# An H3 layer with a gated product, forward and backward: a third weight slab at the start, transposes at fixed places, and a convolution that runs on into the down product

## The chip, the cores and the metric

The kernel runs on one core of a Trainium2 chip. The metric is device time in microseconds (us) of one execution, the median of several. The engines have the profile's names: PE (TensorE, matmuls and transposes), PEld (its weight loads), DVE (VectorE), ACT (ScalarE), POOL (GpSimd) and SP (SyncE, which issues DMAs only). An engine works through its own list of instructions in order; a DMA is issued by an instruction on the list of SP, ACT or POOL.

## The reference

One layer and all its gradients, with 2048 rows, 1024 features (D) and 3584 hidden features (F), in bfloat16:

```python
xn = _layernorm(q)
# A: convolution over the rows
k_shift = sum_t k_pad[:, t:t+S] * shift_k[:, ks-1-t]      # ks = 4
kv = k_shift * v
y = irfft(rfft(kv, 2S) * rfft(ssm_k, 2S))[:, :S] + kv * ssm_D
s = xn * y
# B: gated product
h = (xn @ w_gate) * (xn @ w_up)
g = silu(h @ w_down)
out = q + s * g
```

The outputs are `out` and its gradients for q, k, v, shift_k, ssm_k, ssm_D, w_gate, w_up and w_down, given grad_out.

## The kernel before

Everything is one program whose order is written out by hand. **Stages**, by the trace: 0 to 62 us the layer norm of q and the first units of the gate/up product; to about 512 us the rest of that product with the forward convolution woven into it; to about 700 us the down product with the gates; then the backward products to the end at 1916 us. Only the first three are touched.

**Layer norm and turning.** q comes in chunks of rows, in blocks of 128: (0,1), (1,1), (2,2), (4,4), (8,4), (12,4) as first block and number (L889). `layer_norm` (L565) makes a chunk's statistics on DVE, a square root on ACT (`half_r`, L580), the normalized rows on DVE (L591), and stores them to XNd from POOL's queue. Each block is then turned, by transposes on PE (L597, L608, and L617 in `turn_late`) and a copy on ACT, into XNT, the stationary side of the product. Blocks of chunks 8-11 and 12-15 wait in a list `turn_rows`, which `turn_late` empties after the first block of the next unit (L660).

**Gate/up product.** The weights come in 14 slabs of 256 columns of w_up beside 256 of w_gate (`load_slab`, L547, two DMAs of 512 KB on SP's queue). `gu_unit(sl, b0, n)` (L640) multiplies n row blocks by slab sl: per block 8 matmuls of 512 columns (L656) into one of two PSUM banks of `ps_gu`, a copy on ACT (gut, L658), and a store of gut to GUd from ACT's queue (L72). Later h = up times gate on DVE (hN, L667), its store, its transposes on PE (L689), and a copy on ACT with a store of h transposed. Slabs 0 and 1 are loaded at the start, between the first chunks of rows; the first units alternate between them, as chunks become ready (L927). From slab 2 on, units of four blocks run over all 16.

**Forward convolution.** It is a generator, `conv_forward` (L706), over eight slices (ds) of 128 features. Per slice: transforms of kv (kind 0) and of ssm_k (kind 1), their product, an inverse transform, and a tail of inverse row matmuls (psY, L446) with copies to yf. A transform is matmuls on PE into banks of `ps_cv` (psF), a copy on ACT into SP (L296), and sums on DVE. `fwd4_half` (L249) takes 16 matmuls of 256 columns; `fwd8_half` (L288) 8, with more sums on DVE (`fwd8`, L298). EIGHT (L698) lists the slices and kinds split by eight. `make_pump` (L473) advances the generator: each piece yields a cost, and after every row block `tick` (L944) pumps until the cost done reaches a share of F_TOTAL, set by `cnt` and NT (L942). Within it the order of DVE's instructions is pinned.

**Down product.** `bm_first` (L998) begins the first two row blocks, two matmuls of 512 columns (L994) per 128 hidden features (fc); `late_mm(n)` (L1327) goes on with one such step per n. Accumulators (psbm) lie in `ps_bm` (two) and `ps_bx` (one). `ps_cv` is released ahead of `bm_first`, so all of the convolution's forward transforms must be issued by then. The tail's last four pieces are placed behind steps n = 52, 55, 58 and 61 (L1337). `gate` (L1255) then combines g, y and grad_out on DVE.

Of the kernel before, what the change touches and what calls it, by code (L numbers as in the profile page):

```python
# [19 lines left out]
def build_kernel(  # L20
# [266 lines left out]

    def fwd8_half(x, i, SP, psp, first=None, held=False):  # L288

        pe_us[0] += 0.87  # L290
        for j in range(2):
# [4 lines left out]
            nc.scalar.copy(out=SP[:, :, j], in_=ps[:].rearrange("p s k x -> p s (k x)"))  # L296

    def fwd8(SPs, X, W, C, ahead, late=False):  # L298
# [225 lines left out]
    ps_tr = pool("ps_tr", 1, space=PSUM)  # L524
    ps_gu = pool("ps_gu", 2, space=PSUM)
    ps_st = pool("ps_st", 4, space=PSUM)
# [19 lines left out]

    def load_slab(sl, eng):  # L547
        w = fw.tile([P, DC, 2, SLW], BF16, name="wslab")
        fs = slice(sl * SLW, (sl + 1) * SLW)
        for a, wsrc in ((0, B_w_up), (1, B_w_gate)):  # L550
            last = eng.dma_start(out=w[:, :, a, :], in_=wsrc[:, fs].rearrange("(dc p) f -> p dc f", p=P))
# [11 lines left out]
    turn_rows = []  # L563

    def layer_norm(b0, n, x4):  # L565
# [22 lines left out]
        for i in range(n):  # L588
            b = b0 + i
            q, qi = divmod(b, 4)  # L590
            last = V.tensor_scalar(x4[:, i, :], x4[:, i, :], mv[:, i, 0:1], RSTD[:, b:b + 1], op0=SUB, op1=MUL)  # L591
            if b < 2:
                for hh in range(2):
                    ps = ps_st.tile([P, 4, P], BF16, name="tr")
                    for dc in range(4):
                        d0 = (4 * hh + dc) * P
                        tr_ln[0] = nc.tensor.transpose(ps[:, dc, :], x4[:, i, d0:d0 + P], ident[:])  # L597
                    act_copy[0] = nc.scalar.copy(out=XNT[0][:, 4 * hh:4 * hh + 4, b * P:b * P + P], in_=ps[:])
                if b == 0:
                    with tc.issue_after(tr_ln[0].ins):  # L600
# [5 lines left out]
            ps = ps_st.tile([P, DC, P], BF16, name="tr")  # L606
            for dc in range(DC):
                tr_ln[0] = nc.tensor.transpose(ps[:, dc, :], x4[:, i, dc * P:(dc + 1) * P], ident[:])  # L608
            act_copy[0] = nc.scalar.copy(out=XNT[q][:, :, qi * P:(qi + 1) * P], in_=ps[:])
# [30 lines left out]
    def gu_unit(sl, b0, n, w, tick):  # L640

        if n == 4:
            turn_of[0] += 1
            if turn_of[0] % 3 == 0 and sl < NSL - 2:
                gut = U[5][:, 2048:4096].rearrange("p (a i f) -> p a i f", a=2, i=4)
            else:
                gut = fg.tile([P, 2, 4, SLW], BF16, name="gut")
            hN = fg.tile([P, 2, 4, P], BF16, name="hN", bufs=3)
        else:
            gut = lnp.tile([P, 2, 2, SLW], BF16, name="gut_s", bufs=6)  # L650
            hN = lnp.tile([P, 2, 2, P], BF16, name="hN_s", bufs=6)
        for i in range(n):
            q, qi = divmod(b0 + i, 4)
            ps = ps_gu.tile([P, 512], F32, name="psg")
            for dc in range(DC):
                gu_mm[0] = nc.tensor.matmul(ps[:], XNT[q][:, dc, qi * P:(qi + 1) * P],  # L656
                                            w[:, dc].rearrange("p a f -> p (a f)"), start=(dc == 0), stop=(dc == DC - 1))
            nc.scalar.copy(out=gut[:, :, i], in_=ps[:].rearrange("p (a f) -> p a f", a=2))  # L658
# [43 lines left out]
    conv_state = {"forward": True, "filters": True}  # L702

    y_first = [None]

    def conv_forward():  # L706
# [83 lines left out]
        def half(ds, x, i, first=None):  # L790
            if (ds, int(first is not None)) not in EIGHT:
                return fwd4_half(x, i, cf, ps_cv, first)
            SP = cf.tile([P, 2, 2, 512], F32, name="SP", bufs=2)
            fwd8_half(x, i, SP, ps_cv, first, True)
            return SP

        def transform(ds, kind, sp, X, C, ahead, step):

            if ds == 7 and kind == 1:
                S_["forward"] = False  # L800
            if (ds, kind) in EIGHT:
                W = fwd4_buf(cs)[:].rearrange("p a b c x -> p (a b c) x")
                for n, w in enumerate(fwd8(sp, X, W, C, ahead, True)):
                    if n in (0, 2, 4, 6):
                        step()
# [26 lines left out]
        for ds in range(8):  # L832
# [16 lines left out]
            next(tl, None)  # L849
            room = cf.tile([P, 4, 256], F32, name="room", tag="hx")[:] if eight else None  # L850
            yield from transform(ds, int(ds > 0), sph, HX if ds else KX, room, nop1 if eight else lambda c: h_rows(ds + 1, c),
# [7 lines left out]
            if eight:  # L859
                h_rows(ds + 1, 1)  # L860
            if ds == 7:
                cf.release()
                S_["filters"] = False
            st(HFd[ds], HX[:])
# [14 lines left out]
        for _ in tl:  # L879
# [9 lines left out]
    chunks = [(0, 1), (1, 1), (2, 2), (4, 4), (8, 4), (12, 4)]  # L889
    xs = [(b0, n, u8((4, 6, 7)[b0 // 4 - 1], a=4) if n == 4 else lnp.tile([P, n, D], BF16, name=f"x{b0}")[:])  # L890
          for (b0, n) in chunks]
    for c in xs[0:2]:
# [3 lines left out]
    slabs.append(load_slab(1, nc.sync)[0])  # L896
    for c in xs[3:]:
        ln_load(*c)

# [38 lines left out]
    ps_st.release()  # L938
    ps_cv = pool("ps_cv", 2, space=PSUM)
    pump, drain, step = make_pump(conv, F_TOTAL)  # L940
    cnt = [-5]
    NT = 24 * 8.0 + 33  # L942

    def tick(by=1):  # L944
        cnt[0] += by
        if cnt[0] == -4:
            pump((SHIFT_W + 4.05) / F_TOTAL)
        if cnt[0] >= -2:
            pump((SHIFT_W + (F_TOTAL - SHIFT_W) * (cnt[0] + 6.5) / (NT + 3.5)) / F_TOTAL)

    pump((SHIFT_W + 3.95) / F_TOTAL)
    for i_ in (4, 5):
        gu_unit(1, *xs[i_][0:2], slabs[1], tick)
    for sl in range(2, NSL - 2):
        w, wld = load_slab(sl, nc.sync)
# [50 lines left out]
    assert not conv_state["forward"]  # L1006
# [5 lines left out]
    for p_ in (ps_gu, fg, fw):  # L1012
        p_.release()
# [19 lines left out]
    mh = [pool("mh0", 1, side="right")]  # L1033
    ps_bx = pool("ps_bx", 1, space=PSUM)

# [338 lines left out]
    for bp in range(2, 8):  # L1374
# [18 lines left out]
        for i in range(2):  # L1393
# [7 lines left out]
            gate(2 * bp + i, ps_of[2 * bp + i])  # L1401
    for p_ in (ps_bx, ps_tr, ps_y, ps_bm, mi, mo, mt, mh[1], mh[0]):
        p_.release()
# [363 lines left out]
```

## Time and profile before

| | us |
|---|---|
| median of 3 runs | 1917.38 (1917.29 to 1918.71) |
| profiled execution, its own time | 1918.36 |
| its span | 1916.6 |
| PE busy | 1905.7 |
| DVE busy | 1557.1 |
| ACT busy | 640.0 |
| POOL busy | 334.5 |
| PE, L656 (gate/up product) | 407.3, 1792 matmuls |
| PE, L994 (down product) | 146.0, 672 matmuls |
| PE waiting, 0 to 120 us | 7.0 in 9 waits of the view of waits |

The profile is of one execution. Its strips cut the span into 40 slices of 47.9 us, with the busy share of each in tenths (9 is 90% or more). Groups of instructions are named by line, engine, operation and tiles (out<-in); a wait names what ended an engine's idle time. Matmuls overlap, so their own durations are longer than the time from one start to the next.

### The profile page before, as it was taken

The numbers are of one execution on the slowest core, as the hardware profiler recorded it, in microseconds if no ns is written. First come the engines' busy times: TensorE is split into PE (matmuls) and PEld (weight loads), VectorE is DVE, ScalarE is ACT, GpSimd is POOL, SyncE is SP. The second block draws the span as 40 slices with busy tenths as digits, with TensorE's granted clock in tenths as the row PEclk, the third lists the DMA queues.
The fourth block names the chain that finished last, engine by engine and source line by source line (L and its number), as shares of the span: only waits on it lengthen the run. The fifth ranks groups of instructions, "written<-read, shape, count | busy, mean of one in ns | idle before, by whom it ended". The sixth has DMA issues, their size and how long they took to land. (4 is left out here: it accounts for less than half of the span.)

```text
span 1916.6 us, 27330 instructions
## 1 busy us (share of the span) xinstructions
PE 1905.7 (99%) x10915; PEld 1024.9 (53%) x10915; DVE 1557.1 (81%) x1723; ACT 640.0 (33%) x946; POOL 334.5 (17%) x465
## 2 busy tenths in 40 slices
PE   8999999999999999999999999999999999999999
PEld 5555555545544456666666665664444444444444
DVE  8999999999997556887999999999995205788862
ACT  5864555646433233432222222222222102011121
POOL 5121212111113220001031221111212101111120
PEclk9999999999999999999999999999999999999999
DMA  8776867668679997677887698585787999999962
GB/s 293 271 261 216 265 209 234 211 234 299 237 246 287 316 287 250 205 240 236 269 271 261 220 263 270 180 286 177 217 255 173 206 205 191 184 184 195 193 180 97
DMA packets 425487, 444.28 MB, mean 232 GB/s; under 512 B 268784, under 2 KB 343180, under 8 KB 410896
## 3 DMA queue, kind: packets, MB, share of 16 engines
q1 hardware_dynamic: 367888, 239.03, 46.9%
q0 software_dynamic: 41152, 174.15, 29.1%
q10 hardware_dynamic: 16320, 29.36, 4.1%
q8 instruction: 85, 1.39, 0.3%
q14 instruction: 42, 0.34, 0.1%
HBM read 193.87 MB, written 189.84 MB: 200 GB/s over the span
## 5 line engine op out<-in xcount | busy, mean ns | idle before, releaser
L656 PE MATMUL psg<-wslab,U 128*128 128x512 bf16 x1792 | 407.3, 379 | 3.0 <-DMA wslab<-in_B_w_gate_dram 2.0
L1458 PE MATMUL psb<-U,U 128*128 128x512 bf16 x1792 | 397.1, 379 | 0.0
L1603 PE MATMUL psx<-U,dgut 128*128 128x512 bf16 x1536 | 333.0, 379 | 0.5 <-DVE dxn L213 0.5
L1603 PEld LDWEIGHTS <-dgut 128*128 128x128 bf16 x1792 | 175.3, 98 | 212.1 <-issue 0.8
L1458 PEld LDWEIGHTS <-U 128*128 128x128 bf16 x1792 | 175.2, 98 | 198.0
L656 PEld LDWEIGHTS <-U 128*128 128x128 bf16 x1792 | 172.2, 98 | 187.4 <-issue 2.5
L1441 PE MATMUL psb<-wdt,U 128*128 128x256 bf16 x1792 | 205.6, 273 | 0.0
L213 DVE TENSOR_TENSOR W<-W 128x1024 f32<-128x1024 f32 (+1 forms) x192 | 189.1, 1001 | 4.2
L1441 PEld LDWEIGHTS <-U 128*128 128x128 bf16 x1792 | 175.3, 98 | 29.2
L1541 PE MATMUL psb<-U,U 128*128 128x512 bf16 x816 | 177.3, 379 | 0.0
L1463 ACT CAST wb<-psb 128x512 bf16<-128x512 f32 x112 | 65.6, 586 | 315.4 <-PE psb L1458 310.5
L1208 DVE SCALAR_TENSOR_TENSOR dkp<-dkT,kT 128x1024 bf16<-128x1024 bf16 (+2 forms) x64 | 78.3, 1224 | 104.0 <-DMA dkT<-DKSHd 102.2
L994 PE MATMUL psbm<-U,ht 128*128 128x512 bf16 x672 | 146.0, 379 | 0.0
L1541 PEld LDWEIGHTS <-U 128*128 128x128 bf16 x896 | 87.4, 98 | 104.3
L658 ACT CAST gut<-psg 128x512 bf16<-128x512 f32 x156 | 91.3, 588 | 120.0 <-PE psg L656 119.1
L1635 ACT ACTIVATE dx_t<-dxn 128x1024 bf16<-128x1024 f32 x15 | 15.9, 1057 | 324.2 <-DVE dxn L213 320.3
L994 PEld LDWEIGHTS <-ht 128*128 128x128 bf16 x672 | 65.6, 98 | 78.0
L213 DVE TENSOR_TENSOR U<-U,dht 128x2048 bf16<-128x2048 bf16 x56 | 68.3, 1221 | 46.4 <-ACT dht L1443 46.4
L1443 ACT CAST dht<-psb 128x512 bf16<-128x512 f32 x112 | 65.6, 587 | 116.3 <-PE psb L1441 116.3
L66 POOL DMA_DIRECT2D Hd<-hN x54 | 37.1, 686 | 292.3 <-DVE hN L213 289.4
L1582 ACT CAST wbs<-psb 128x512 bf16<-128x512 f32 x51 | 29.9, 586 | 145.4 <-PE psb L1541 137.3
L213 DVE TENSOR_TENSOR W<-SP 128x1024 f32<-128x1024 f32 x64 | 74.5, 1219 | 2.5 <-ACT SP L296 1.7
(261 smaller groups left out, 2386.3 us busy)
## 6 DMA issues: line engine op xcount, KB each, us to landing
U<-GUd SPq DMA_DIRECT2D x28, 1024.0 KB, 8.7
DGd<-U SPq DMA_DIRECT2D x28, 1024.0 KB, 6.5
GUd<-gut ACTq DMA_DIRECT2D x39, 512.0 KB, 5.5
out_dram<-wb SPq DMA_DIRECT2D x112, 128.0 KB, 4.8
U<-Hd SPq DMA_DIRECT2D x14, 1024.0 KB, 5.9
Hd<-hN POOLq DMA_DIRECT2D x54, 256.0 KB, 4.2
HTd<-hT SPq DMA_DIRECT2D x52, 256.0 KB, 3.9
ht<-HTd SPq DMA_DIRECT2D x18, 512.0 KB, 7.7
```

Of the source, the lines that this page charges most:

```text
L66: ins = nc.gpsimd.dma_start(out=out, in_=in_)
L213: pinned(V.tensor_tensor(o, a, b, op))
L656: gu_mm[0] = nc.tensor.matmul(ps[:], XNT[q][:, dc, qi * P:(qi + 1) * P], w[:, dc].rearrange("p a f -> p (a f)"), start=(dc == 0), stop=(dc ...
L658: nc.scalar.copy(out=gut[:, :, i], in_=ps[:].rearrange("p (a f) -> p a f", a=2))
L994: mm = nc.tensor.matmul(ps[:, dh * 512:(dh + 1) * 512], ht(fc)[:, i * P:(i + 1) * P], WD[fc // 4][:, fc % 4, dh * 512:(dh + 1) * 512], sta ...
L1208: ins = V.scalar_tensor_tensor(prod[:].rearrange("p r d -> p (r d)")[:, lo:H], dkT[:, 0, lo:H], 1.0, kT[:, 0, 13 + m + lo:13 + m + H], op0 ...
L1441: nc.tensor.matmul(ps[:, x * SLW:(x + 1) * SLW], DBMT[2 * hf + g][:, dc, (b % 4) * P:(b % 4 + 1) * P], wdt[:, dc, :], start=(dc == 0), sto ...
L1443: nc.scalar.copy(out=dht[:, 2 * e:2 * e + 2].rearrange("p b f -> p (b f)"), in_=ps[:])
L1458: nc.tensor.matmul(ps[:], XN[b // 4][:, b % 4, dc * P:(dc + 1) * P], dgus[b // 8][:, :, b % 8], start=(b == 0), stop=(b == NB - 1))
L1463: nc.scalar.copy(out=wb[:, dc % 2].rearrange("p a f -> p (a f)"), in_=ps[:])
L1541: nc.tensor.matmul(ps, h[:, f, b, :], DBM[b // 4][:, b % 4, dh * 512:(dh + 1) * 512], start=(b == 0), stop=(b == NB - 1))
L1603: nc.tensor.matmul(ps[:, dh * 512:(dh + 1) * 512], t[n][:, f, i * P:(i + 1) * P], WGU[n][:, f, dh * 512:(dh + 1) * 512], start=(n == 0 and ...
```

## The change

1. **Split.** (4, 0) joins EIGHT: slice 4's transform of kv is split by eight.
2. **Third slab.** Slab 2 is loaded at the start too, into the buffer U7, behind slab 1 and ahead of chunk 4-7. Slabs 0 to 2 come in halves over d, four DMAs of 256 KB each. Chunk 4-7 comes in two DMAs; chunk 12-15 is loaded later, into the room of the first chunks. Units (0,2), (1,2), (2,2), as (chunk number, slab), are done with the first ones. hN_s has 8 buffers in place of 6.
3. **Turns.** The transposes of a chunk are put off into `turn_next` or `turn_rows`, and issued behind a given unit or block (TURN_AT).
4. **Running on.** The convolution's banks are taken by `Banks` in turn; in the down product it keeps one, and the first accumulator has the other. The last transform's four matmul parts are kept in `cv_parts` and issued between steps of `bm_first`. `ps_bx` goes, `ps_gu` lies on the other side, and `ps_bm` has one accumulator. The room for an eight-way transform moves to krow. NT goes from 33 to 37 over 192, cnt from -5 to -4; the last tail pieces stand behind steps 82, 85, 88 and 91.

```diff
-    def fwd8_half(x, i, SP, psp, first=None, held=False):
+    def fwd8_half(x, i, SP, psp, first=None, held=False, parts=None):
...
+        for j in range(2):
+            if parts is None:
+                part(j)
+            else:
+                parts.append(lambda j=j: part(j))
...
+        n = DC // 2 if sl < 3 else DC
+        for d0 in range(0, DC, n):
+            for a, wsrc in ((0, B_w_up), (1, B_w_gate)):
+                last = eng.dma_start(out=w[:, d0:d0 + n, a, :],
+                                     in_=wsrc[d0 * P:(d0 + n) * P, fs].rearrange("(dc p) f -> p dc f", p=P))
...
+        elif b0 == 4:
+            for r in (0, 2):
+                ld(x4[:, r:r + 2, :], xq[:, c, r0 + r:r0 + r + 2, :])
...
+                else:
+                    turn_next.append(((1, 0), turn_first))
...
-            if b0 >= 8:
+            if b0 >= 4:
                 turn_rows.append((x4[:, i, :], q, qi))
...
+            turn_next.append(((0, 2), turn_second))
...
+    TURN_AT = ((1, 2, 1), (0, 4, 2), (0, 8, 1))
...
-            if i == 0:
+            if (sl, b0, i) in TURN_AT:
                 turn_late()
...
-    EIGHT = ((0, 0), (0, 1), (5, 0), (6, 0), (7, 0), (7, 1))
+    EIGHT = ((0, 0), (0, 1), (4, 0), (5, 0), (6, 0), (7, 0), (7, 1))
...
+    class Banks:
+        n, alone = 0, False
+
+        def tile(self, shape, dt, name):
+            self.n = 0 if self.alone else 1 - self.n
+            return ps_cv.tile(shape, dt, name=name, tag=f"psF{self.n}")
...
+            while cv_parts:
+                cv_parts.pop(0)()
...
+    slabs.append(load_slab(2, nc.sync, u8(7, "p (c a f) -> p c a f", c=DC, a=2))[0])
+    ln_load(*xs[3])
+    ln_load(*xs[4])
...
+        if i == 2:
+            ln_load(*xs[5])
...
-        for i_, sl in ([(0, 0)], [(1, 0), (0, 1), (1, 1)], [(2, 0), (2, 1)], [(3, 0), (3, 1)], [(4, 0)], [(5, 0)])[i]:
+        for i_, sl in ([(0, 0)], [(1, 0), (0, 1), (1, 1), (0, 2), (1, 2)], [(2, 0), (2, 1), (2, 2)], [(3, 0), (3, 1)],
+                       [(4, 0)], [(5, 0)])[i]:
+            while turn_next and turn_next[0][0] == (i_, sl):
+                with tc.issue_after(gu_mm[0].ins):
+                    turn_next.pop(0)[1]()
...
-    cnt = [-5]
-    NT = 24 * 8.0 + 33
+    cnt = [-4]
+    NT = 24 * 8.0 + 37
...
-    def bm_first(fcs):
+    def bm_first(fcs, blocks=(0, 1)):
         for fc in fcs:
-            for i in range(2):
+            for i in blocks:
                 mm = bm_mm(pss[i], lambda fc: HT0[fc // 16][:, fc % 16], i, fc)
-            if fc % 2 == 1:
-                tick()
+            if fc % 2 == 1 or len(blocks) == 1:
+                if cv_parts:
+                    cv_parts.pop(0)()
+                if fc % 4 == 3 or len(blocks) == 2:
+                    tick()
...
-    ps_cv.release()
-    ps_bm = pool("ps_bm", 2, side="right", space=PSUM)
-    pss = [ps_bm.tile([P, D], F32, name="psbm") for i in range(2)]
-    with tc.issue_after(bm_first(range(4)).ins):
+    cv_banks.alone = True
+    bm_bank = lambda n: ps_cv.tile([P, D], F32, name="psbm", tag=f"psF{n}")
+    pss.append(bm_bank(1))
+    bm_first(range(4), (0,))
+    ps_gu.release()
+    ps_bm = pool("ps_bm", 1, side="right", space=PSUM)
+    pss.append(ps_bm.tile([P, D], F32, name="psbm"))
+    with tc.issue_after(bm_first(range(4), (1,)).ins):
         flush()
...
-            ps_of[b] = (ps_bx if b % 3 == 2 else ps_bm).tile([P, D], F32, name="psbm")
-        with tc.issue_after(inv_mm[0].ins) if b < 5 else nullcontext():
+            ps_of[b] = ps_bm.tile([P, D], F32, name="psbm") if b % 3 == 1 else bm_bank(b % 3 // 2 ^ 1)
+        with tc.issue_after(inv_mm[0].ins) if n < at[3] + 4 or b < 5 else nullcontext():
...
-    at = (52, 55, 58, 61)
+    at = (82, 85, 88, 91)
```

More of the change, by code (lines that the diff above doesn't have):

```diff
@@ L286, in stt, with part @@
             tc.keep_in_program_order(ins)
-    def fwd8_half(x, i, SP, psp, first=None, held=False):
+    def fwd8_half(x, i, SP, psp, first=None, held=False, parts=None):
         pe_us[0] += 0.87
-        for j in range(2):
+        def part(j):
             r = 2 * i + j
@@ L524, in build_kernel @@
     ps_tr = pool("ps_tr", 1, space=PSUM)
-    ps_gu = pool("ps_gu", 2, space=PSUM)
+    ps_gu = pool("ps_gu", 2, side="right", space=PSUM)
     ps_st = pool("ps_st", 4, space=PSUM)
@@ L545, in build_kernel, with load_slab @@
     lnp = pool("lnp", 1)
-    def load_slab(sl, eng):
-        w = fw.tile([P, DC, 2, SLW], BF16, name="wslab")
+    def load_slab(sl, eng, w=None):
+        if w is None:
+            w = fw.tile([P, DC, 2, SLW], BF16, name="wslab")
         fs = slice(sl * SLW, (sl + 1) * SLW)
-        for a, wsrc in ((0, B_w_up), (1, B_w_gate)):
-            last = eng.dma_start(out=w[:, :, a, :], in_=wsrc[:, fs].rearrange("(dc p) f -> p dc f", p=P))
+        n = DC // 2 if sl < 3 else DC
[3 more added lines that the diff above has]
+                                     in_=wsrc[d0 * P:(d0 + n) * P, fs].rearrange("(dc p) f -> p dc f", p=P))
         return w, last
@@ L563, in build_kernel @@
     turn_rows = []
+    turn_next = []
     def layer_norm(b0, n, x4):
@@ L592, in layer_norm, with turn_first, turn_second @@
             if b < 2:
[L593 to L598, printed above, removed]
+                def turn_first(b=b):
+                    for hh in range(2):
+                        ps = ps_st.tile([P, 4, P], BF16, name="tr")
+                        for dc in range(4):
+                            d0 = (4 * hh + dc) * P
+                            tr_ln[0] = nc.tensor.transpose(ps[:, dc, :], x4[:, 0, d0:d0 + P], ident[:])
+                        act_copy[0] = nc.scalar.copy(out=XNT[0][:, 4 * hh:4 * hh + 4, b * P:b * P + P], in_=ps[:])
                 if b == 0:
+                    turn_first()
                     with tc.issue_after(tr_ln[0].ins):
                         keep_busy(10)
+                else:
+                    turn_next.append(((1, 0), turn_first))
                 continue
-            if b0 >= 8:
+            if b0 >= 4:
                 turn_rows.append((x4[:, i, :], q, qi))
                 continue
[L606 to L609, printed above, removed]
+            def turn_second(i=i, q=q, qi=qi):
+                ps = ps_st.tile([P, DC, P], BF16, name="tr")
+                for dc in range(DC):
+                    tr_ln[0] = nc.tensor.transpose(ps[:, dc, :], x4[:, i, dc * P:(dc + 1) * P], ident[:])
+                act_copy[0] = nc.scalar.copy(out=XNT[q][:, :, qi * P:(qi + 1) * P], in_=ps[:])
+            turn_next.append(((0, 2), turn_second))
         c, r0 = divmod(b0, 8)
         return last, root, st(xnn[:, c, r0:r0 + n, :], x4[:, 0:n, :])
+    TURN_AT = ((1, 2, 1), (0, 4, 2), (0, 8, 1))
     def turn_late():
@@ L650, in gu_unit @@
             gut = lnp.tile([P, 2, 2, SLW], BF16, name="gut_s", bufs=6)
-            hN = lnp.tile([P, 2, 2, P], BF16, name="hN_s", bufs=6)
+            hN = lnp.tile([P, 2, 2, P], BF16, name="hN_s", bufs=8)
         for i in range(n):
@@ L697, in build_kernel @@
     ht_st = [None]
-    EIGHT = ((0, 0), (0, 1), (5, 0), (6, 0), (7, 0), (7, 1))
+    EIGHT = ((0, 0), (0, 1), (4, 0), (5, 0), (6, 0), (7, 0), (7, 1))
     INV8 = (2, 4, 5, 6, 7)
     SHIFT_W = 8 * 2.3
-    conv_state = {"forward": True, "filters": True}
+    conv_state = {"filters": True}
+    class Banks:
[3 more added lines that the diff above has]
+            return ps_cv.tile(shape, dt, name=name, tag=f"psF{self.n}")
+    cv_banks = Banks()
+    cv_parts = []
     y_first = [None]
@@ L791, in half @@
             if (ds, int(first is not None)) not in EIGHT:
-                return fwd4_half(x, i, cf, ps_cv, first)
+                return fwd4_half(x, i, cf, cv_banks, first)
             SP = cf.tile([P, 2, 2, 512], F32, name="SP", bufs=2)
-            fwd8_half(x, i, SP, ps_cv, first, True)
+            fwd8_half(x, i, SP, cv_banks, first, True, cv_parts if cv_banks.alone else None)
             return SP
         def transform(ds, kind, sp, X, C, ahead, step):
-            if ds == 7 and kind == 1:
-                S_["forward"] = False
+            while cv_parts:
+                cv_parts.pop(0)()
             if (ds, kind) in EIGHT:
@@ L803, in transform @@
                 for n, w in enumerate(fwd8(sp, X, W, C, ahead, True)):
+                    if (ds, kind, n) == (7, 1, 2):
+                        cf.release()
+                        S_["filters"] = False
                     if n in (0, 2, 4, 6):
@@ L849, in conv_forward @@
             next(tl, None)
-            room = cf.tile([P, 4, 256], F32, name="room", tag="hx")[:] if eight else None
+            room = None
+            if eight:
+                room = krow[:].rearrange("p a b d -> p (a b d)")[:, NB * P:2 * NB * P].bitcast(F32).rearrange("p (a x) -> p a x", a=4)
             yield from transform(ds, int(ds > 0), sph, HX if ds else KX, room, nop1 if eight else lambda c: h_rows(ds + 1, c),
@@ L860, in conv_forward @@
                 h_rows(ds + 1, 1)
-            if ds == 7:
-                cf.release()
-                S_["filters"] = False
             st(HFd[ds], HX[:])
@@ L889, in build_kernel @@
     chunks = [(0, 1), (1, 1), (2, 2), (4, 4), (8, 4), (12, 4)]
-    xs = [(b0, n, u8((4, 6, 7)[b0 // 4 - 1], a=4) if n == 4 else lnp.tile([P, n, D], BF16, name=f"x{b0}")[:])
-          for (b0, n) in chunks]
+    x_own = lnp.tile([P, 4, D], BF16, name="x_own")
+    xs = [(b0, n, u8((4, 6)[b0 // 4 - 1], a=4) if b0 in (4, 8) else x_own[:, b0 % 4:b0 % 4 + n, :]) for (b0, n) in chunks]
     for c in xs[0:2]:
@@ L896, in build_kernel @@
     slabs.append(load_slab(1, nc.sync)[0])
-    for c in xs[3:]:
-        ln_load(*c)
+    slabs.append(load_slab(2, nc.sync, u8(7, "p (c a f) -> p c a f", c=DC, a=2))[0])
+    ln_load(*xs[3])
+    ln_load(*xs[4])
     ang, ang_ins = angles(tg)
@@ L938, in build_kernel @@
     ps_st.release()
-    ps_cv = pool("ps_cv", 2, space=PSUM)
+    ps_cv = pool("ps_cv", 1, space=PSUM)
     pump, drain, step = make_pump(conv, F_TOTAL)
-    cnt = [-5]
-    NT = 24 * 8.0 + 33
+    cnt = [-4]
+    NT = 24 * 8.0 + 37
     def tick(by=1):
         cnt[0] += by
-        if cnt[0] == -4:
-            pump((SHIFT_W + 4.05) / F_TOTAL)
         if cnt[0] >= -2:
             pump((SHIFT_W + (F_TOTAL - SHIFT_W) * (cnt[0] + 6.5) / (NT + 3.5)) / F_TOTAL)
-    pump((SHIFT_W + 3.95) / F_TOTAL)
+    pump((SHIFT_W + 4.05) / F_TOTAL)
     for i_ in (4, 5):
         gu_unit(1, *xs[i_][0:2], slabs[1], tick)
-    for sl in range(2, NSL - 2):
+    for b0 in (4, 8, 12):
+        gu_unit(2, b0, 4, slabs[2], tick)
+    for sl in range(3, NSL - 2):
         w, wld = load_slab(sl, nc.sync)
@@ L996, in bm_mm @@
         return mm
-    def bm_first(fcs):
+    pss = []
+    def bm_first(fcs, blocks=(0, 1)):
         for fc in fcs:
-            for i in range(2):
+            for i in blocks:
                 mm = bm_mm(pss[i], lambda fc: HT0[fc // 16][:, fc % 16], i, fc)
-            if fc % 2 == 1:
-                tick()
-        return mm
-    assert not conv_state["forward"]
-    ps_cv.release()
-    ps_bm = pool("ps_bm", 2, side="right", space=PSUM)
-    pss = [ps_bm.tile([P, D], F32, name="psbm") for i in range(2)]
-    with tc.issue_after(bm_first(range(4)).ins):
+            if fc % 2 == 1 or len(blocks) == 1:
[3 more added lines that the diff above has]
+                    tick()
+        return mm
+    cv_banks.alone = True
[6 more added lines that the diff above has]
+    with tc.issue_after(bm_first(range(4), (1,)).ins):
         flush()
-    for p_ in (ps_gu, fg, fw):
+    for p_ in (fg, fw):
         p_.release()
@@ L1033, in build_kernel @@
     mh = [pool("mh0", 1, side="right")]
-    ps_bx = pool("ps_bx", 1, space=PSUM)
+    assert not cv_parts
     ddo = const.tile([P, 8], BF16, name="ddo")
@@ L1401, in build_kernel @@
             gate(2 * bp + i, ps_of[2 * bp + i])
-    for p_ in (ps_bx, ps_tr, ps_y, ps_bm, mi, mo, mt, mh[1], mh[0]):
+    for p_ in (ps_cv, ps_tr, ps_y, ps_bm, mi, mo, mt, mh[1], mh[0]):
         p_.release()
```

## The prediction

> **What bounds the kernel now.** I read the page's shares and strips first, to learn which engine sets the time and where another one comes near it.
>
> ```profile
> span 1916.6 us, 27330 instructions
> ...
> PE 1905.7 (99%) x10915; PEld 1024.9 (53%) x10915; DVE 1557.1 (81%) x1723; ACT 640.0 (33%) x946; POOL 334.5 (17%) x465
> ...
> PE 8999999999999999999999999999999999999999
> ...
> DVE 8999999999997556887999999999995205788862
> ```
>
> TensorE (PE) is busy 99% of the span; the one slice below 9 is the first (a slice is 47.9 us). VectorE (DVE) is at 9 in slices 2 to 12, about 48 to 575 us: the forward convolution beside the gate/up product. So time can be saved by fewer matmuls, or in the first 50 us; between those, DVE stands ready to become the bound. Second, the waits of PE in the first 120 us:
>
> ```profile
> PE psg L656 <- DMA wslab<-in_B_w_gate_dram: 2.0, 2, 1.0
> PE tr L532 <- POOL ident masks.py:199: 1.4, 1, 1.4
> PE tr L608 <- DVE U L591: 0.9, 1, 0.9
> PE psg L656 <- ACT gut L658: 0.8, 2, 0.6
> PE tr L617 <- DVE U L591: 0.7, 1, 0.7
> ```
>
> Columns: total us, times, longest. Two waits for gate slabs, two for normalized rows (U, line 591), two for copies out of PSUM. Third, the busy times by stretch (us, PE, PEld, DVE, ACT, POOL, clock, DMA share, GB/s):
>
> ```profile
> 10.00:20.00 10.00, 8.79 (x59) 4.45 (x58) 8.34 (x21) 5.03 (x9) 3.97 (x5) 1.00 1.09 390
> 20.00:30.00 10.00, 9.05 (x70) 5.05 (x69) 9.49 (x28) 6.14 (x11) 5.97 (x9) 1.00 0.76 285
> 30.00:40.00 10.00, 8.69 (x70) 4.92 (x69) 9.52 (x27) 6.98 (x14) 5.32 (x8) 1.00 0.82 257
> 80.00:500.00 420.00, 419.40 (x2588) 231.78 (x2587) 416.08 (x390) 238.02 (x337) 71.56 (x101) 1.00 0.71 237
> ```
>
> From 10 to 40 us PE loses 3.5 us. From 80 to 500 us PE is busy for 419.40 and DVE for 416.08: both are full. The granted clock is 1.00 throughout, so a matmul's price doesn't move: from start to start 512 columns take 216 ns, 256 columns 109, 128 columns 56 in the timeline. Against these, the matmuls up to 60 us start 5.45 us late in all: 1.16 before the second matmul of the first slab (its gate half lands at 9.13), 0.40 (ACT's copy), 1.14 (gate of slab 1, landing at 14.58), 1.11 and 0.89 (rows of chunks 4-7 and 8-11), 0.75 (ACT's copy). Last, DVE's timeline, with the idle time before an entry in brackets:
>
> ```profile
> 72.27 4.63 DVE L213 TENSOR_TENSOR W<-SP 128x1024 f32<-128x1024 f32 x4 [1.74 <-ACT SP L296]
> ...
> 562.51 0.69 DVE L213 TENSOR_TENSOR so<-U,U 128x1024 bf16<-128x1024 bf16 x1 [3.81 <-issue]
> ```
>
> In DVE's waits between these two points nothing else stands: DVE runs for 490 us without a gap, and whatever is added to it there moves all behind it. PE's small late starts from 50 to 550 us, 0.05 to 0.23 us each, are 4 to 5 us together: the two engines already touch.
>
> **Fewer matmuls.** Slice 4's transform of kv (shifted k times v) by eight: 8 matmuls of 256 columns per half in place of 16, two halves, so 16 x 0.109 = **-1.75 us** of PE. DVE pays: an eight-way transform takes 15.7 us in DVE's timeline (492.5 to 509.5 less two hN products), a four-way one 9.6, so +6.1 us. Hidden only where DVE has room.
>
> **DVE's stretch.** The first `W<-SP`, at 72.27, had waited 1.74 us for PE's first transform. In the order built for the changed kernel, PE has 68.4 us of work ahead of that transform where it had 60.9 (four more groups of eight matmuls stand before it), while DVE's shift work ends at about 72 as now: so DVE waits there some 7.5 us longer, and the convolution starts later against PE. From there to the last transposes of the product h (hN, which read DVE) I added up both engines' instructions in the built orders, each with its duration in this trace. Before: PE 437.8, DVE 441.0 us. After: PE 425.4, DVE 433.4 us. DVE's surplus grows from 3.2 to 8.0, though four steps of the convolution run on into the down product; not every us of it reaches PE, since before 0.8 us of DVE's sum lay in overlaps. I take **+4.2 us**, about 1.8 at the second half of a kv transform and the rest at the last hN transposes. Below: 0, if DVE's order leaves the added work behind what PE asks for; above: 4.8, the whole difference. What is late next has room. The last inverse transforms go from steps 52-61 of the down product to 82-91, 30 x 0.43 = 13 us later, so gates start later; but DVE is busy 22.80 of 40 us at 600-640 and waits 46.1 us for ACT's sig, which waits for PE, until 700, so nothing is added. The down product still has three accumulators, two of them now the convolution's banks; the one that is free later costs nothing as long as a block's 12.1 us cover ACT's copies (0.59 us for 512 columns).
>
> **The start.** Slabs in halves: the first four matmuls need half a slab, some 8.2 us instead of 9.26, gain 0.9. The turns of x1's rows and slab 2's units stand in front of the waits for chunks 4-7 and 8-11: 1.11 + 0.89 go, less 0.3 left in small waits; slab 1's wait of 1.14 goes too, since units of three slabs give PE 1.7 us each: together **-3.75 us**, if nothing new comes. What comes is on ACT's own list, in program order there. (a) The store of the first unit's gut now stands ahead of the copy of x1's second transposes, and in the built order it carries a wait for the semaphore that slab 1's last quarter counts on (eight semaphores are dealt out in turn, and two more DMAs per slab have shifted them). That quarter lands at about 14.6, as slab 1 does now; the copy is done at about 15.7, where PE would have needed it at 12.65: **+3.0 us**. Now the same store is issued at 12.79 without waiting. (b) The square root of chunk 4-7's statistics stands ahead of the copy of a unit, which frees the PSUM bank for the unit two on. Slab 2 (1 MB at 300 to 400 GB/s: 2.6 to 3.5 us) now lands ahead of that chunk, whose root ran at 24.01 and will at 26 to 28; PE asks at 26, so 1.7 to 5 us with the copy behind it, and I take 1.7, since rows and statistics of the first two rows can start on the first half. The stores after the first wait for slab 2's quarters, which land before them. Start: -3.75 + 3.0 + 1.7 = **+0.95**, bounds -3.75 and +4.25.
>
> Two rules of the Trainium skill speak here. The first wslab halves of 512 KB land at 7.40 and 9.13 us, 1.73 apart. "DMA: Bandwidth & Descriptors", section "Measured", says to batch transfers to 1 MiB, and its anatomy section gives some 2.0 us fixed per DMA: six more DMAs would be an estimated +12 us if each paid alone. The trace speaks against that, as 512 KB follow within less than the fixed part. The same page's anatomy section says that a semaphore wait of a DMA happens on the sequencer that issues it, ahead of dispatch, which would make (a) real; no store in the trace of before waits so. Without (a) the sum would be 3.0 lower.
>
> **Sum**: -1.75 + 4.2 + 0.95 = **+3.4 us**. The profiled execution took 1918.36 (span 1916.6 and 1.8 around it), 0.98 over the median of 1917.38; so 1921.8 in its terms and **1920.8** at the median. About 0.2%, 3.8 us, is what a measurement can tell from no change: 1913.5 to 1921.2.
>
> **Rivals.**
> - A, the forecast, 1918.5 to 1923.0: chance 0.40, two fifths of it above 1921.2.
> - B, faster: the start keeps its -3.75 and DVE's added work falls behind PE's needs. -5.5, **1911.9**. For: all 3.5 us lost in 10 to 40 us have a named cause that the edit addresses. Against: ACT's order and the 8.0 against 3.2. Chance 0.22.
> - C, slower: ACT in order as the bound of the start, both stalls at their upper ends (root at 28, with copy and next bank behind it) and DVE's stretch as forecast: -1.75 + 4.2 + 4.25 = +6.7, **1924.1**. It decides once the root comes after 27 us, when PE has emptied its two banks. For: DVE is busy 9.49 of 10 us at 20-30. Chance 0.15.
> - M, one half only: a good start with a full DVE (-1.75 - 3.75 + 4.2 = -1.3) or a late ACT with DVE covered (-0.8): 1916.1 to 1916.6. Chance 0.18.
> - D, that it doesn't do what it says: slab and turns change nothing, the convolution hides; the 16 matmuls remain, -1.75, 1915.6. Chance 0.05.
>
> Faster: most of B and a little of its neighbours, 0.22. Slower: C and two fifths of A, 0.31. The rest, 0.47, is within. The range goes from B's lower side to just above C, 1911.0 to 1924.5.
>
> **What would show it.** Right: 16 matmuls fewer in PE's count; PE idle at about 13 to 15.7 us for ACT's copy behind a store issued only near 14.6; no wait for normalized rows in chunks 4-11; DVE's gap at the first `W<-SP` grown to some 9 us and none after it until the gates; PE waiting 2 to 4 us for hN near 510 us. Wrong: a store issued at once after its copy, or a DVE with gaps in 90 to 500 us. If DVE's gap-free stretch ends before PE asks for the last hN, step two falls and B or M holds; a new wait in the down product after step 91 would say that the PSUM banks cost something.

## The result, and the profile after

The changed kernel takes 1929.39 us (median of 6, 1925.39 to 1933.76), the kernel before 1918.15 beside it: a ratio of 1.0054, interval [1.004, 1.0067]. It is **11.2 us slower** by the medians; 1920.8 was forecast, with a range to 1924.5. The profiled execution is the longest of the six (1933.76, span 1932.0), so its stalls add up to more than the median shows: +15.4 us between the two profiled executions.

First, shares and strips of the page after:

```profile
span 1932.0 us, 27342 instructions
...
PE 1908.6 (99%) x10899; PEld 1022.8 (53%) x10899; DVE 1563.3 (81%) x1737; ACT 639.6 (33%) x948; POOL 334.6 (17%) x467
...
DVE  7899999999998555888799999999996204788862
```

PE has its 16 matmuls less (10915 to 10899) and DVE 6.2 us more, as forecast. DVE's strip is still at 9 from the third slice to the twelfth, but its second slice fell from 9 to 8: DVE comes later into its long stretch.

All waits of PE after (total us, times, longest):

```profile
PE psg L679 <- ACT U L681: 5.9, 2, 3.2
PE psbm L1036 <- DMA ht<-HTd: 4.4, 1, 4.4
PE psg L679 <- ACT U L613: 3.6, 2, 3.2
PE tr L538 <- POOL ident masks.py:199: 1.4, 1, 1.4
PE psF L235 <- ACT SP L257: 1.2, 1, 1.2
PE psF L235 <- DVE kv L213: 1.1, 1, 1.1
PE tr L612 <- DVE x_own L605: 0.8, 2, 0.5
PE psg L679 <- ACT gut L681: 0.4, 1, 0.4
```

Before, the same view has 6.0 us in 8 waits up to 120 us, and not 7.0 in 9 as the table above says. The waits for weight slabs, and for the rows of chunks 4-7 and 8-11, are gone. In their place stand two copies of ACT that came late (U, L613 and L681), a late load (ht), and two waits on the convolution (SP, kv).

The most telling line is DVE's first sum, which stood at 72.27 with 1.74 us of waiting, and the first gate (so), at 562.51 before:

```profile
83.31 4.63 DVE L213 TENSOR_TENSOR W<-SP 128x1024 f32<-128x1024 f32 x4 [4.72 <-ACT SP L297]
...
584.42 0.69 DVE L213 TENSOR_TENSOR so<-U,U 128x1024 bf16<-128x1024 bf16 x1 [7.66 <-issue]
```

DVE's chain starts 11.0 us later. Behind that it has one wait of 0.3 us up to the convolution's last piece, where it had none, and the gates start 21.9 us later. The first sum waits for ACT's copy of PE's first transform, and PE begins this transform 11.0 us later (first before, then after):

```profile
69.62 0.27 PE L235 MATMUL psF<-hx,TF 128*128 128x256 bf16 x1
...
80.62 0.27 PE L235 MATMUL psF<-hx,TF 128*128 128x256 bf16 x1
```

Where PE stalls for long, the clock in the records falls too. Busy times by stretch, after (the clock is the third from last):

```profile
16.00:18.00 2.00, 1.87 (x5) 0.74 (x6) 1.64 (x7) 0.18 (x2) 0.00 (x0) 0.50 1.12 320
...
645.00:650.00 5.00, 0.80 (x2) 0.28 (x3) 1.71 (x3) 0.00 (x0) 0.00 (x0) 0.70 1.03 413
650.00:655.00 5.00, 5.00 (x16) 1.92 (x15) 4.93 (x9) 0.00 (x0) 2.08 (x4) 0.62 1.16 317
```

At 650 to 655 us PE is "busy" all the time and does only 16 matmuls of 512 columns, where 23 fit at 216 ns.

A matmul is late by what its start lies further behind the start of the one before than the price of that one (216, 109 or 56 ns). Where PE waits ahead of matmuls of 512 columns, this is some 0.16 us more than the view of waits has, since a matmul's own duration runs on into the wait. Late time after less before, in the profiled executions: 0 to 100 us +3.3; 100 to 500 us +7.3; 600 to 700 us +6.9; elsewhere -0.6; the 16 matmuls -1.75. That makes +15.2, of which the slow matmuls behind long waits are 1.4 + 1.6 + 2.3 = 5.3.

### The profile page after: what moved, and what is told of

It reads as the page before. It is cut to its first block, busy times and chain, and to the rows that moved or that the text cites. A ratio compares the mean times of both kernels' runs of the same rounds, so it can differ in the third digit from the quotient of the medians.

```text
span 1932.0 us, 27342 instructions
## 1 busy us (share of the span) xinstructions
PE 1908.6 (99%) x10899; PEld 1022.8 (53%) x10899; DVE 1563.3 (81%) x1737; ACT 639.6 (33%) x948; POOL 334.6 (17%) x467
## 4 chain that ended last, share of the span: by engine, by line
PE 86%; DVE 7%; DMA 4%; issue 2%; ACT 1%; SPq 0%; POOL 0%; ACTq 0%; DVEq 0%
PE psb L1508 20%; PE psx L1653 20%; PE psg L679 13%; PE psb L1491 10%; PE psb L1591 9%; PE psbm L1036 7%; PE psF L235 2%; DVE W L213 1%; PE psY L452 1%; DMA HTd<-hT 1%; DVE KX L213 1%; PE tr L712 1%; DMA yf_t<-YFd 1%; PE psY L1202 1%; PE psx L1591 1%
## 5 line engine op out<-in xcount | busy, mean ns | idle before, releaser
L679 PE MATMUL psg<-wslab,U 128*128 128x512 bf16 x1664 | 382.0, 381 | 9.9 <-ACT U L681 5.9
L681 ACT CAST gut<-psg 128x512 bf16<-128x512 f32 x152 | 89.1, 587 | 128.6 <-PE psg L679 123.6
```

## The experiments

Each kernel is timed beside the kernel before; the ratio and its interval are to that, and differences in us to the changed kernel are between medians. Marked cuts (...) leave out the rest of an edit. "First sum" is DVE's first `W<-SP`, "chain" the time from there to the end of the convolution's last piece.

**The parts one by one.** What the four parts do is separated by taking the split, the run-on and the new start alone or in pairs. Where the split went in without the run-on, the convolution had to be paced a little faster.

`split40_alone`:

```diff
-    EIGHT = ((0, 0), (0, 1), (5, 0), (6, 0), (7, 0), (7, 1))
+    EIGHT = ((0, 0), (0, 1), (4, 0), (5, 0), (6, 0), (7, 0), (7, 1))
...
-    NT = 24 * 8.0 + 33
+    NT = 24 * 8.0 + 32
```

> The kernel before with one part of the change: slice 4's kv transform split by eight, the convolution still ending ahead of the down product (192 + 32 row blocks in place of 192 + 33 for its pace, so that the longer DVE work fits). Theory (the loss is a few separate stalls that the start and the late tail bring; the split is not one of them): 16 matmuls fewer, -1.75 us, and 0 to 2 us of PE stalls for DVE: -1.75 to +0.5 us. Rival (DVE is the bound and the split's 6.1 us of DVE work come out on PE): +2.5 to +4.5 us, and waits of PE for DVE or SP of 4 us or more between 80 and 515 us.

Measured: 1928.43, 1.0055 [1.004, 1.007]. The theory fell here and the rival was even too small: the split, with its pace, costs 10.7 us by the medians. PE's waits of this kernel between 80 and 560 us:

```profile
PE tr L689 <- DVE hN L213: 3.5, 1, 3.5
PE psF L235 <- ACT SP L257: 1.7, 2, 1.5
PE psF L235 <- DVE kv L213: 1.7, 2, 1.3
PE tr L689 <- ACT hx L755: 1.5, 1, 1.5
PE psY L446 <- ACT yf L773: 1.2, 1, 1.2
```

In the same stretch the kernel before waits for none of these. The longest is for DVE's last hN product, which ended at 521.7 us in place of 512.4. That the waits for ACT's copies (SP, hx, yf) hang on the same chain of DVE is my reading; they were not traced back.

`old_start` (the hunks for slab 2, halves, turns and units taken back):

```diff
-    slabs.append(load_slab(2, nc.sync, u8(7, "p (c a f) -> p c a f", c=DC, a=2))[0])
...
-    NT = 24 * 8.0 + 37
+    NT = 24 * 8.0 + 40
```

> The changed kernel with the start of the kernel before (two slabs, whole slabs, old turns), pace adapted to the four more row blocks; the split and the run-on into the down product are kept. Theory: PE's stall of 3.3 us at 12.6 us and of 2.9 us at 64.6 us go, the stall for ht at 644 us (4.6 us and about 2.1 us of slow matmuls behind it) stays: +4 to +7 us against the kernel before. Rival (the start is the whole loss): 0 to +1 us. Rival (DVE's work): +2.5 us and more, without a stall for ht.

Measured: 1919.71, 1.0006 [0.9997, 1.0016], below the theory's range and nearest to the first rival: 9.7 us of the changed kernel's time go with the old start. The run-on takes the split's cost back almost whole; ht is still waited for (2.6 us), and so is a copy of ACT (gut) near 361 us, 2.8 us.

`new_start` (the kernel before with the start's hunks and the split):

```diff
...
-    cnt = [-5]
-    NT = 24 * 8.0 + 33
+    cnt = [-4]
+    NT = 24 * 8.0 + 29
...
```

> The kernel before with the new start (third slab, halves, fixed turns) and the split, but its convolution ends ahead of the down product as before (pace 192 + 29) and the tail stands at steps 52 to 61. Theory: the stall at 12.6 us stays (3.3 us and 1.4 us of slow matmuls) and so may that at 64.6 us (2.9 us); before's 5.45 us of late starts go for the most part; no stall for ht near 644 us: +1 to +5 us. Rival (the start gains, the late tail is the whole loss): -3 to -5 us.

Measured: 1936.28, 1.0096 [1.0081, 1.0111]. Both expectations were too low. First sum at 82.4 us, last hN product at 530.4; PE waits for SP, kv, hN and hx 13.2 us in all. There is no stall near 644 us. That alone does not put this stall down to the late tail: the tail stands at its old steps here, but PE too gets the last hN 13.5 us later than in the changed kernel, and so asks for ht later.

`no_split` (the changed kernel with EIGHT as before):

```diff
-    EIGHT = ((0, 0), (0, 1), (4, 0), (5, 0), (6, 0), (7, 0), (7, 1))
+    EIGHT = ((0, 0), (0, 1), (5, 0), (6, 0), (7, 0), (7, 1))
```

> The changed kernel without its split (slice 4's kv transform by four again): 16 matmuls more, 6.1 us less DVE work. Theory (run-on makes room for the split, so that DVE's work costs nothing any more; the loss is ACT held by DMAs at the start and in the middle, and ht loaded late): +0.5 to +2 us against the changed kernel (1929.4). Rival (the split's DVE work is still the loss, as it is without the run-on): 4 us or more below the changed kernel, and PE's waits for SP and kv at 143 and 193 us gone.

Measured: 1924.29, 1.0034 [1.0024, 1.0044]: 5 us below the changed kernel, though the two intervals just touch, and PE's waits at 143 and 193 us are gone. The rival's number and sign hold. So run-on seems to make room for the split with the old start, and not with the new one.

`run_on_alone` (old start, EIGHT as before):

```diff
...
-    cnt = [-4]
-    NT = 24 * 8.0 + 37
+    cnt = [-5]
+    NT = 24 * 8.0 + 40
...
```

> The kernel before with the run-on alone (old start, no split; pace 192 + 40). Theory: DVE gets room before the last transposes of h, so the small stalls of 4 to 5 us from 50 to 550 us fall, but the stall for ht near 638 us (2.7 us and slow matmuls behind it) comes, as the gates start 10 us or more later: -2 to +4 us against the kernel before. Rival (run-on costs nothing): -3 to -1 us with no stall near 640 us. A third: it only helps with the split in, then within 1 us of before.

Measured: 1918.62, 1.0006 [0.9996, 1.0015]. The theory's range and the third both hold it. DVE now has idle time in its chain (some 5 us more than before), the last hN ends at 506.8, and ht is waited for 1.0 us.

Together, the measured ratios to before:

| | old start | new start |
|---|---|---|
| no split, no run-on | 1 | not tried |
| split | 1.0055 | 1.0096 |
| run-on | 1.0006 | 1.0034 |
| split and run-on | 1.0006 | 1.0054 |

The new start costs 0.3 to 0.5% in every row.

**Single stalls of the changed kernel.** `store_behind` and `no_v3` each take one away.

`store_behind`:

```diff
...
+            if put_next and i_ > 0:
+                with tc.issue_after(act_copy[0].ins):
+                    put_next.pop(0)()
```

> The changed kernel, with the store of the first unit's gut issued behind the copy of x1's second transposes in place of ahead of it; the number and order of DMAs on the other queues are the same. Theory (the store's wait for slab 1's last quarter holds up that copy): the stall at 12.6 us falls from 3.3 us to under 0.7 and the slow matmuls behind it go: 3 to 5 us less than the changed kernel, whose median is 1929.4. Rival (PE would wait for the slab anyway): within 1 us of the changed kernel.

Measured: 1931.81, 1.0072 [1.0056, 1.0087]; no gain. The stall at 12.6 us did fall, to 1.0 us, but then ACT's square root (half_r) became the next to hold a copy, as ACT's timeline of this kernel shows:

```profile
21.68 0.52 ACTq L72 DMA_DIRECT2D GUd<-gut_s  x1
26.84 0.21 ACT L595 ACTIVATE half_r<-vpe 128x4 f32<-128x4 bf16 x1 [5.19 <-DMA GUd<-gut_s]
26.96 0.57 ACT L682 CAST gut_s<-psg 128x512 bf16<-128x512 f32 x1
```

PE stalls 3.1 us at 24.4 for the copy at 26.96, with slow matmuls behind it. The profile names the store of gut as what ended half_r's wait; chunk 4-7's statistics on DVE feed half_r too, and which of them was last I did not separate.

`no_v3`:

```diff
-                        cld_v(v, i, dp * 256, 256)
+                    if dp != 3:
+                        cld_v(v, i, dp * 256, 256)
```

> The changed kernel without the load of the last quarter of v (1 MB in four DMAs on POOL's queue, issued at 349 to 353 us), so this part of kv and all that follows from it is not the reference's; the rest of the program is the same. Theory (a burst of slab, k, v and stores fills all DMA engines from 340 to 365 us; the store of h transposed lies behind the slab, and ACT's next copy waits for its buffer): the slab lands 2.5 to 3.3 us earlier than 22 us after its issue, the stall at 366 us falls from 3.3 to under 1 us and the 2 us of slow matmuls go: 3 to 5 us below the changed kernel. Rival (a wait for a semaphore whatever the load): the stall stays within 1 us of 3.3.

This kernel leaves a quarter of v out and is good for its timing alone. Measured: 1930.97, 1.0065 [1.0049, 1.0081]; no gain either, yet the theory's stall did go. The stall at 366 us is gone and the slab landed 17.3 us after its issue in place of 22.4. But PE's waits from 300 us on are now these:

```profile
PE psbm L1037 <- DMA ht<-HTd: 5.0, 1, 5.0
PE tr L712 <- DVE hN L213: 2.7, 1, 2.7
```

The second is new: the changed kernel does not wait for hN. **What PE gained at 366 us (3.3 us and 1.6 of slow matmuls) it gave back at 512 us** (2.9 us late and 1.8 of slow matmuls), waiting for DVE's last hN. That is what made me drop the theory of separate stalls. DVE's chain, begun late, says when PE may leave the gate/up product; a stall of PE that lies beside it costs little by itself.

**The chain's start.** `slab2_behind` moves 32 matmuls behind the first transform:

```diff
-        for i_, sl in (..., [(1, 0), (0, 1), (1, 1), (0, 2), (1, 2)], [(2, 0), (2, 1), (2, 2)], ...)[i]:
+        for i_, sl in (..., [(1, 0), (0, 1), (1, 1)], [(2, 0), (2, 1)], ...)[i]:
...
-    for b0 in (4, 8, 12):
+    for b0 in (0, 4, 8, 12):
         gu_unit(2, b0, 4, slabs[2], tick)
```

> The changed kernel, with slab 2 still loaded at once and in halves, but all its units behind the convolution's first transform, as four units of four blocks (32 matmuls less ahead of that transform; pace 192 + 41). In the changed kernel DVE's first sum of a transform starts at 83.3 us and the rest of DVE's chain takes 489.8 us from there to the last piece of the convolution. Theory (this chain sets the time, so its start counts one for one): the start falls to 76 to 79 us, where DVE's shift work ends, the convolution's last piece from 573 to 566 to 569 us, and the time by 4 to 7 us against the changed kernel (1929.4), though waits for rows come back in the first 50 us. Rival (stalls of PE count one by one): those waits add 1 to 3 us and nothing is gained: 1930 to 1932.

Measured: 1920.72, 1.0015 [1.0006, 1.0024]: 8.7 us below the changed kernel. The stall at 13 us is still in it (2.8 us late and slow matmuls). DVE's first sum and PE's waits from 60 to 700 us, of this kernel:

```profile
74.91 4.63 DVE L213 TENSOR_TENSOR W<-SP 128x1024 f32<-128x1024 f32 x4 [1.93 <-ACT SP L297]
```

```profile
PE psbm L1039 <- DMA ht<-HTd: 1.8, 1, 1.8
```

The first sum is 8.4 us earlier, and the waits for SP and kv, and those for ACT's copies at 64.6 and 366 us, are gone with it. For the one at 366 us an early chain is not enough: old_start, whose first sum stands at 72.5 us, has its like near 361. The chain is as long as in the changed kernel (489.2 against 489.8 us), so its start moved all behind it.

**The tail.** `tail_72`:

```diff
-    at = (82, 85, 88, 91)
+    at = (72, 75, 78, 81)
```

> The changed kernel with the last tail pieces behind steps 72, 75, 78 and 81 in place of 82 to 91: psY comes 4.3 us earlier, just behind DVE's last piece at 573 us. Theory (late gates hold back SP's loads of ht): ht is issued some 4 us earlier, and the stall of 4.6 us near 644 us with the 2.1 us of slow matmuls behind it shrinks to under 1 us: 4 to 7 us below the profile of the changed kernel, 3 to 6 us at the median. Rival (ht is late because of the full DMA queues alone): the stall stays over 3 us, within 1 us.

Measured: 1926.2, 1.0046 [1.0031, 1.0061], 3.2 us less than the changed kernel; no wait for ht. The two intervals overlap, so it is the wait that shows the effect and not the median. SP's queue shows how the gates hold ht back in the changed kernel:

```profile
625.70 10.00 SPq L1434 DMA_TRANSPOSE U<-DBMd  x1
635.79 0.52 SPq L61 DMA_DIRECT2D do_t<-in_grad_out_dram  x1
636.41 0.40 SPq L61 DMA_DIRECT2D xn_t<-XNd  x1
636.90 0.75 SPq L61 DMA_DIRECT2D yf_t<-YFd  x1
637.70 2.07 SPq L61 DMA_DIRECT2D ht<-HTd  x3
```

and in the kernel before:

```profile
602.53 11.32 SPq L1384 DMA_TRANSPOSE U<-DBMd  x1
613.95 1.65 SPq L61 DMA_DIRECT2D ht<-HTd  x3
```

A transposing DMA, which reads what the gates stored, holds the queue for 10 us, and ht stands behind it. Gates 21.9 us later put this group 23 us later, and the three ht loads are issued 7 us before PE wants the first of them; the first takes 11.5 us from issue to landing, so PE waits 4.4 us. The same load took 10.1 us in the kernel before and 7.1 us in `tail_72`, where it is issued at 633.48. 7 us is too little for any of these three, so without the late issue there is no such wait; how much of the 4.4 us the full DMA engines, the rival, add was not separated.

`old_start_tail` and `run_on_tail`, the same edit on the two kernels with the old start:

```diff
-    at = (82, 85, 88, 91)
+    at = (69, 72, 75, 78)
```

> Old start, with split and run-on, and the last tail pieces behind steps 69, 72, 75 and 78 in place of 82 to 91. DVE's last piece ends at 566 us there, psY came at 572.6 and the first gate at 578.5. Theory (late gates hold back ht): psY at 566 to 568, first gate at 572 to 574, the stall of 2.7 us at 638 us gone: 2 to 4 us below the 1919.7 of old_start, so 1915.5 to 1918. Rival (ht late for other reasons): within 1 us of 1919.7.

> Old start and run-on without the split, the last tail pieces behind steps 66, 69, 72 and 75. DVE's last piece ends at 561 us there and the first gate came at 574.5. Theory: first gate at 567 to 569, the stall of 1.1 us at 634 us gone: 0.5 to 2 us below the 1918.6 of run_on_alone, about the kernel before. Rival: within 0.5 us of 1918.6.

Measured: `old_start_tail` 1919.52, 1.0005 [0.9994, 1.0017]; `run_on_tail` (66 to 75) 1916.75, 0.9993 [0.9984, 1.0002]. The first gate is where it was expected (569.2, even earlier, and 567.7), and ht is not waited for in either. With the split the median didn't follow, and the rival's number holds: its profile shows a new wait of 2.7 us in the backward part (1609 us, psx for dxn), which had cost run_on_alone 2.2 us too and which I did not trace. `run_on_tail` is the fastest kernel here, 1.2 us under the kernel before in the median; its interval takes in 1, so it is not shown to be faster than before, only than the changed kernel.

`joined` (new start as in slab2_behind and store_behind, run-on, no split, tail at 68 to 77):

> What the runs so far point to, in one kernel: the changed kernel with slab 2's units behind the convolution's first transform, the first store of gut behind the copy of x1's turns, no split of slice 4, and the last tail pieces behind steps 68 to 77. Theory (DVE's chain from its first sum sets the time, and with it waits of PE in the first 50 us count again): the first sum at 72 to 74 us, no stall over 1.5 us behind 10 us, none near 635 us; below run_on_tail's 1916.75, at 1913.5 to 1916.5. Rival (the new start is worth nothing): 1916.5 to 1919.

Measured: 1920.94, 1.0016 [1.0007, 1.0025]. First sum at 74.9 us. Neither expectation holds: the new start costs even without its extra units ahead of the first sum. PE's waits of this kernel from 10 to 120 us:

```profile
PE psg L680 <- ACT gut_s L682: 2.2, 2, 1.9
PE psg L680 <- ACT gut L682: 1.9, 1, 1.9
PE psg L680 <- DMA wslab<-in_B_w_gate_dram: 1.2, 1, 1.2
PE psg L680 <- ACT U L630: 0.6, 1, 0.6
PE psg L680 <- ACT U L614: 0.5, 1, 0.5
```

With a last wait of 0.2 us that makes 6.6 us, where the kernel before waits 3.6 us in all. The third slab takes the waits for rows away, and the waits for ACT's copies give back more. The first sum, the chain (489.1 us) and the median are those of slab2_behind within 0.3 us: together the store, the split and the earlier tail do not show in the time here.

## Why the prediction was wrong, point by point

The decisive view is DVE's chain in all these kernels (us, from DVE's timelines and the spans; each row is one execution, the changed kernel's the longest of its six):

| | first sum | chain | last hN ends | first gate | span |
|---|---|---|---|---|---|
| before | 72.3 | 482.7 | 512.4 | 562.5 | 1916.6 |
| split40_alone | 72.2 | 489.8 | 521.7 | 572.7 | 1926.0 |
| old_start | 72.5 | 493.3 | 509.5 | 578.5 | 1921.6 |
| new_start | 82.4 | 490.6 | 530.4 | 581.1 | 1934.7 |
| changed | 83.3 | 489.8 | 516.8 | 584.4 | 1932.0 |
| no_split | 85.8 | 482.7 | 514.6 | 580.9 | 1923.9 |
| slab2_behind | 74.9 | 489.2 | 507.9 | 575.3 | 1918.1 |
| run_on_tail | 72.2 | 488.5 | 506.8 | 567.7 | 1915.0 |
| run_on_alone | 72.1 | 488.5 | 506.8 | 574.5 | 1920.1 |
| old_start_tail | 72.6 | 490.1 | 506.5 | 569.2 | 1919.4 |
| joined | 74.9 | 489.1 | 510.1 | 571.8 | 1918.6 |
| store_behind | 82.8 | 489.4 | 516.0 | 583.4 | 1927.0 |
| no_v3 | 82.5 | 488.9 | 515.2 | 582.5 | 1930.7 |
| tail_72 | 86.1 | 488.9 | 518.8 | 582.1 | 1927.1 |

The six kernels with the run-on and a first sum from 72 to 75 us span 1915.0 to 1921.6 us, the five with one from 82 to 86 us 1923.9 to 1932.0. Within a group the first sum does not order them.

- **Fewer matmuls**: right, 16 less, -1.75.
- **DVE's stretch, +4.2**: DVE's sum was right. From first sum to last hN I had 433.4 us; the trace has 516.8 - 83.3 = 433.5, and the last hN ends 4.4 us later than before. Where it would come out was wrong: I had PE waiting 2 to 4 us for hN near 510, and PE is 0.2 us late near 518, since it had already lost the time at 143 (1.35), 193 (1.2) and 366 us (3.3 and 1.6 of slow matmuls). As late time of PE it is +7.3, above my upper bound of 4.8. The stall at 366 us, ACT's copy behind a slow slab, was in no term.
- **The start, +0.95**: term (a) was right, 3.3 us measured against 3.0, and the store was issued at 14.86, when slab 1's last quarter landed (14.78). Term (b) did not show, as (a) had already held PE; it showed in store_behind, 3.1 us. Two things were in no term: the slow matmuls behind (a), and ACT, which is busy with tables and turns and keeps PE waiting for 2.9 us more at 64.6. So PE is 3.3 us later than before up to 100 us, within the bounds, and reaches the first transform 11.0 us later, where I had 7.5 and the start's 0.95. The first sum waits for this transform, and that is its whole lateness. "DVE's shift work ends at about 72 as now" failed too, but did not set the first sum: the work ended at 78.6, after a wait of 2.8 us for k, and so DVE's gap was 4.7 us and not the 9 that I named as a sign. With the units of slab 2 behind the transform (slab2_behind) it ended at 73.0.
- **The step that failed most in the profiled execution: "nothing is added" behind the convolution.** I let 13 us of later gates vanish in DVE's idle time of 600 to 700 us. DVE had that time; SP's queue had not. The gates feed a transposing DMA, ht stands behind it, and PE was 4.6 us late with 2.3 us of slow matmuls: +6.9 in the profiled execution, where I had 0, and about 3 at the median by tail_72. I looked at DVE and ACT, not at SP. At the median the rest of the miss of 8.6 us is in the start and DVE's stretch, which I had at +5.15 together: taking the start back (old_start) or moving 32 matmuls behind the first transform (slab2_behind) saves 9.7 and 8.7 us.
- **A term left out**: the slow matmuls behind long waits, 5.3 us in this execution. I had taken the clock of 1.00 as fixed.
- **Rivals**: C had the direction and part of the mechanism (ACT at the start, DVE's stretch), at 1924.1. None had ht, and none reached 1929.4.
- **A price that was cited and not used**: the Trainium skill ("DMA: Bandwidth & Descriptors", section "Anatomy of one DMA — SWDGE (gpsimd) path") gives its fixed 2.0 us or so for a DMA that POOL issues. The slabs are issued by SP, and no run here prices the fixed part of a DMA.

What stays open: why the new start without its extra units ahead (joined) is still 4 us over run_on_tail, though its first sum is only 2.7 us later and PE's late starts up to 50 us are some 2.3 us more; why the load of ht took 11.5 us; and the wait at 1609 us that comes and goes in kernels that do not differ there.

## What to carry to other kernels

Where a second engine runs without a gap beside a busy PE, price an edit by that engine's chain: when it starts, how long it is, and what its end releases. Work and stalls ahead of its first instruction are paid there, while a stall of PE beside it can be exchanged for another and not added, as no_v3 shows for one. A stage that is moved later must be followed into each DMA queue that it feeds, since a queue in order passes the delay on to loads that have nothing to do with it.

## What the runs showed of the hardware

PE at half clock after waits: in the profiled executions of these kernels PE started 2.3 us or more late 23 times (counted from start to start, from 9 us on). Behind 20 of these the granted clock is at 0.50 for a while, and 7 to 14 matmuls take twice their time (426 in place of 216 ns for 512 columns), at once or within 1.5 us: +1.4 to 2.8 us each. Behind three (2.63, 2.72 and 2.89 us) and behind all 23 late starts of 1.3 to 2.3 us it is not. The Trainium skill ("TensorE: Matmul & The Clock Gate", section "Why this matters for your kernels") advises no idle gaps over some 3 us; in these traces late starts from 2.4 us on were already enough in most cases.

The time from issue to landing varies by a factor of two at much the same share of the DMA engines: a slab's half of 512 KB took 22.4 us in the changed kernel (share 0.97 to 1.06 from 340 to 365 us), and 10.7 us in the kernel before (0.84 to 1.06 from 335 to 350 us). Without 1 MB of v beside it (no_v3) it was 17.3 us; what makes up the rest was not separated.
